# gMLP z2 in nine groups of eight column units, with batch-norm statistics for its mean and variance

## The chip, the cores and the metric

One core of one Trainium2 chip runs the whole program. The metric is the device time of one execution in microseconds (us), start to end, lower is better. The core has five engines that run their own instruction streams and wait for each other by semaphores: TensorE (PE in the profile, with its weight loads as PEld), VectorE (DVE), ScalarE (ACT), GpSimd (POOL) and SyncE (SP, which here only starts transfers). Matrix products land in PSUM, which has eight banks of 512 float32 columns; everything else lives in SBUF, 128 partitions wide.

## The reference

Four layers, A B A B, on x of 2048 rows and 576 columns. A is a dilated local attention; B is a gated MLP (gMLP). The change is inside B only:

```python
def _layernorm(x, axis=-1, eps=1e-05):
    m = jnp.mean(x, axis=axis, keepdims=True)
    v = jnp.var(x, axis=axis, keepdims=True)
    return (x - m) / jnp.sqrt(v + eps)

def _B_ref(x, w_in, w_sp, b_sp, w_out):
    B, S, D = x.shape                      # 1, 2048, 576
    F = w_in.shape[-1]                     # 4608
    Fh = F // 2                            # 2304
    z = _gelu(jnp.einsum('bsd,df->bsf', x, w_in))
    z1 = z[..., :Fh].copy()
    z2 = _layernorm(z[..., Fh:], axis=-1)
    g = jnp.einsum('ts,bsf->btf', w_sp, z2) + b_sp[None, :, None]
    return jnp.einsum('bsf,fd->bsd', z1 * g, w_out)

x = x + _B_ref(_layernorm(x, axis=-1), B_w_in, B_w_sp, B_b_sp, B_w_out)
```

So z2 is, for every one of the 2048 rows, 2304 columns of Gelu of a product with 576 terms, then normalized over those 2304 columns.

## The kernel before

`layer_B` runs three phases. The first makes z2 and stores its normalized form in `Z`; the second walks over nine pairs of feature blocks, and for each makes z1 (`z1`) and multiplies `Z` by w_sp (`gate`); the third multiplies by w_out. Only the first phase is changed, lines 778 to 876.

**Tiles.** Rows go in 16 row tiles of 128 (`NS`). The 576 terms go as chunks c = 0 to 3 of 128, full height on the array, and c = 4, the last 64. In `xnT` and `win2` the last chunk stands twice, in partitions 0 to 63 and 64 to 127, so that two half-height matmuls can use the two halves of the array; `z_mm` (L814) gives each of them its half by `tile_position`. The 2304 columns of a row tile are four units of 512 and one of 256, in three PSUM allocations: two `H_tile`s of two banks (`pz`) and one `PT_tile` of one bank (`pzs`). There are two H buffers and four PT buffers, together the eight banks.

**Order on TensorE for a row tile** (L822 to L829): the full-height chunks of units 0 and 1, then chunk 4 of all five units (a lone one stays over), then the full-height chunks of units 2 to 4.

**Behind it.** ACT empties the banks by Gelu into `zp` (L831; 1024, 1024 and 256 columns), with running sums in `z_sums`. For the mean square, DVE squares the first 1536 columns (L833) and ACT the other 768 (L835, Square); both write the squares into `spare`, the tenth block of `Z`, and keep only the sums. Five one-column operations on DVE (L838 to L846) make mean and variance, POOL takes the power -1/2 (L848) and makes -mean x rstd (L850). `p1_norm` writes the normalized row: DVE 2048 columns (L858), POOL the last 256 (L860). It is called for row i-1 after row i's main part.

**Buffers.** `zp` has three buffers, so row i's first Gelu waits for both norms of row i-3. `Z` takes over memory in which the attention layer keeps `stg`, from which the last transposes into `xnT` (L252, helper `ln_T`) still read when phase one begins. The space of `zp` is used again by the second phase (w1, `z1T`, `g_tmp`).

**Order.** The attention layer's instructions are issued in a hand-set order (`manual_schedule`); layer B's are put in order by the framework's scheduler. SP's queue holds, in order: the last transposes into `xnT`, the first w1 load, the four transposing loads of w_sp (L777, `Wq`), then more w1. POOL's queue holds the last LayerNorm rows of the attention (L245), the load of the gate's bias (`bsp`, L80, which reuses the buffers `ln_xn` that the last transposes read), then row 0's rstd and so on. `run_deferred` issues the last row's transpose.

In the second phase, one z1 block (L907) is eight units of 512 columns with the same chunks: four units' full-height chunks, chunk 4 of all eight, the other four units' full-height chunks. A gate (L931) reads all 16 row tiles of `Z`, row 15 in its sixteenth matmul.

Of the kernel before, what the change touches and what calls it, by code (L numbers as in the profile page):

```python
# [9 lines left out]
ACT = mybir.ActivationFunctionType  # L10
ALU = mybir.AluOpType
AX = mybir.AxisListType
f32 = mybir.dt.float32
bf16 = mybir.dt.bfloat16
# [4 lines left out]
P = 128  # L19
# [7 lines left out]
PADL = 16  # L27
KO = PADL - HALO
EPS = 1e-5
# [36 lines left out]
class K:  # L66
# [682 lines left out]
    def layer_B(self, li):  # L749
        nc, tc, cfg = self.nc, self.tc, self.cfg  # L750
        S, NS, Fh, NJ, NB, NQ = cfg.S, cfg.NS, cfg.Fh, cfg.NJ, cfg.NB, cfg.NQ
# [7 lines left out]
        Z = zu_cm.__enter__().tile([P, NB + 1, NS, 256], bf16, name="Z")  # L759
        spare = Z[:, NB].rearrange("p a b -> p (a b)")  # L760
# [8 lines left out]
        p1 = p1_cm.__enter__()  # L769
# [3 lines left out]
        def win2(c):  # L773
            return win2a[:, c, :] if c < NPF else win2b[:, c - NPF, :]

        def load_W(q):
            nc.sync.dma_start_transpose(out=Wq[q][:], in_=self.B_w_sp[q * 512:(q + 1) * 512, :])  # L777
        cchunks = []
        c0 = 0
        while c0 < Fh:  # L780
            cn = min(1024, Fh - c0)
            cchunks.append((c0, cn))
            c0 += cn
        ncch = len(cchunks)
        SQ_D = (Fh * 2 // 3) // 256 * 256
        units = []
        for ci, (c0, cn) in enumerate(cchunks):
            for sub in range((cn + 511) // 512):
                units.append((ci, c0, sub, min(512, cn - sub * 512)))
        bsp = self.bsp  # L790
        w1_0 = spare[:, Fh:Fh + 1280].rearrange("p (c n) -> p c n", n=256)
        p2s = []
# [2 lines left out]
        def load_w1(jj):  # L795
            w1 = w1_0 if jj == 0 else p2s[0].tile([P, 5, 256], bf16, name="w1")
            w1s[jj] = w1
            cs = slice(jj * 256, (jj + 1) * 256)
            self.dma(w1[:, 0:4, :], self.B_w_in[0:512, cs].rearrange("(c p) n -> p c n", p=P), eng=nc.sync)
            for r in (0, 64):  # L800
                self.dma(w1[r:r + 64, 4, :], self.B_w_in[512:576, cs], eng=nc.sync)
        zst = {}

        def p1_main(i):
            zp = p1.tile([P, Fh], bf16, name="zp", bufs=3)
            sums = p1.tile([P, ncch + 2], f32, name="z_sums", bufs=3)
            pzvs = []
            for ci, (c0, cn) in enumerate(cchunks):
                if cn > 512:
                    pzvs.append(self.H_tile("pz")[:].rearrange("p a b -> p (a b)"))  # L810
                else:
                    pzvs.append(self.PT_tile([P, 512], f32, "pzs")[:, :])

            def z_mm(u, c, start, stop):  # L814
                ci, c0, sub, w = units[u]
                r0, r1 = (0, P) if c < 4 else (64 * (u % 2), 64 * (u % 2) + 64)
                nc.tensor.matmul(pzvs[ci][:, sub * 512:sub * 512 + w],  # L817
                                 lhsT=self.xnT[r0:r1, c, PADL + i * P:PADL + (i + 1) * P],
                                 rhs=win2(c)[r0:r1, c0 + sub * 512:c0 + sub * 512 + w],
                                 start=start, stop=stop, tile_position=(r0, 0))  # L820
            nu = len(units)
            for u in range(2):  # L822
                for c in range(4):
                    z_mm(u, c, c == 0, False)
            for u in range(nu):
                z_mm(u, 4, u >= 2, u < 2)
            for u in range(2, nu):
                for c in range(4):
                    z_mm(u, c, False, c == 3)  # L829
            for ci, (c0, cn) in enumerate(cchunks):  # L830
                nc.scalar.activation(out=zp[:, c0:c0 + cn], in_=pzvs[ci][:, 0:cn],  # L831
                                     func=ACT.Gelu_apprx_tanh, accum_out=sums[:, ci:ci + 1])
            nc.vector.tensor_tensor_reduce(out=spare[:, 0:SQ_D], in0=zp[:, 0:SQ_D], in1=zp[:, 0:SQ_D], scale=1.0,  # L833
                                           scalar=0.0, op0=ALU.mult, op1=ALU.add, accum_out=sums[:, ncch:ncch + 1])
            nc.scalar.activation(out=spare[:, SQ_D:Fh], in_=zp[:, SQ_D:Fh], func=ACT.Square,  # L835
                                 accum_out=sums[:, ncch + 1:ncch + 2])
            mean = p1.tile([P, 1], f32, name="z_mean", bufs=3)
            nc.vector.tensor_reduce(out=mean[:], in_=sums[:, 0:ncch], axis=AX.X, op=ALU.add)  # L838
            nc.vector.tensor_scalar_mul(out=mean[:], in0=mean[:], scalar1=1.0 / Fh)
            msq = p1.tile([P, 1], f32, name="z_msq", bufs=3)  # L840
            nc.vector.scalar_tensor_tensor(out=msq[:], in0=mean[:], scalar=mean[:, 0:1], in1=self.eps_t[:],
                                           op0=ALU.mult, op1=ALU.subtract)
            sq = p1.tile([P, 1], f32, name="z_sq", bufs=3)
            nc.vector.tensor_tensor(out=sq[:], in0=sums[:, ncch:ncch + 1], in1=sums[:, ncch + 1:ncch + 2], op=ALU.add)
            rstd = p1.tile([P, 1], f32, name="z_rstd", bufs=3)
            nc.vector.scalar_tensor_tensor(out=rstd[:], in0=sq[:], scalar=1.0 / Fh, in1=msq[:],  # L846
                                           op0=ALU.mult, op1=ALU.subtract)
            nc.gpsimd.tensor_tensor(out=rstd[:], in0=rstd[:], in1=self.neg_half[:], op=ALU.pow)  # L848
            nmr = p1.tile([P, 1], f32, name="z_nmr", bufs=3)
            nc.gpsimd.tensor_scalar(out=nmr[:], in0=mean[:], scalar1=rstd[:, 0:1], scalar2=-1.0,  # L850
                                    op0=ALU.mult, op1=ALU.mult)
            zst[i] = (zp, mean, rstd, nmr)

        def p1_norm(i):
            zp, mean, rstd, nmr = zst.pop(i)
            nb = NB - 1
            zv = zp[:].rearrange("p (b c) -> p b c", c=256)
            nc.vector.tensor_scalar(out=Z[:, 0:nb, i, :], in0=zv[:, 0:nb, :], scalar1=mean[:, 0:1],  # L858
                                    scalar2=rstd[:, 0:1], op0=ALU.subtract, op1=ALU.mult)
            nc.gpsimd.tensor_scalar(out=Z[:, nb, i, :], in0=zv[:, nb, :], scalar1=rstd[:, 0:1],  # L860
                                    scalar2=nmr[:, 0:1], op0=ALU.mult, op1=ALU.add)

        for i in range(NS):
            self.run_deferred(upto_row=(i + 1) * P)
            p1_main(i)
            if i == 0:
                self.run_deferred()
            if i == min(2, NS - 1):
                for q in range(NQ):
                    load_W(q)  # L870
                load_w1(0)
            if i == min(6, NS - 1):
                self.dma(bsp, self.B_b_sp.partition_broadcast(P), eng=nc.gpsimd)
            if i >= 1:
                p1_norm(i - 1)
        p1_norm(NS - 1)
        p1_cm.__exit__(None, None, None)
        self.right["pf_cm"].__exit__(None, None, None)
        self.right = None
# [114 lines left out]
        if NS >= 2 and JL > 0:  # L994
            accs = []
            for i in range(2):
                ht = self.H_tile("po2")
# [87 lines left out]
```

## Time and profile before

| What | us |
|---|---|
| median of three runs | 1185.04 |
| the three runs | 1183.01, 1185.39, 1185.04 |
| the profiled execution | 1182.29 |
| its span on the core | 1180.5 |
| first gMLP layer: first pz matmul, first z1 matmul | 127.93, 204.56 |
| second gMLP layer: the same | 709.94, 786.12 |
| one z1 block (40 matmuls) | 7.99 |

The profile is of one execution. A row of the table of groups reads: source line, engine, operation, what it writes and reads with shapes, count; then the total busy time and the mean of one in ns; then the idle time of the engine just before these instructions and what ended it. A timeline row begins with start and length in us; idle time before it and its releaser stand in brackets. "PEq" and the like are the engines' sequencers. The order of instructions on each engine, which the prediction also uses, is that of the built programs.

### The profile page before, as it was taken

Reading aid. Unit: us, or ns where it says so; the run is one execution under the profiler, and the core shown is the slowest. Engines: PE = TensorE matmul, PEld = TensorE weight load, DVE = VectorE, ACT = ScalarE, POOL = GpSimd, SP = SyncE. Lnnn points to the kernel's source line nnn. Section 1 sums busy time; section 2 is a strip of 40 time slices with the busy share of each in tenths; the row PEclk is TensorE's granted clock in tenths of the full one; section 3 lists DMA queues with packets and bytes.
Section 4 is the critical chain, followed back from the end, with each engine's and each line's share of the span. In section 5 each row is a group of like instructions: output and inputs, shape, how many; then the busy total and the mean of one; then the engine's idle time right before and its main releaser. Section 6 shows DMA issues by size and latency. Waiting matters only on the chain.

```text
span 1180.5 us, 20534 instructions
## 1 busy us (share of the span) xinstructions
PE 1169.8 (99%) x8406; PEld 622.2 (53%) x8406; DVE 553.0 (47%) x1232; ACT 377.3 (32%) x621; POOL 285.8 (24%) x383
## 2 busy tenths in 40 slices
PE   9999999999999999999999999999999999999998
PEld 5567544444444444457755774444444444444677
DVE  9778677323333322335556896753322333332321
ACT  5588677111110111102257786770111110111000
POOL 4768784000000000001153787830000000000000
PEclk9999999999999999999999999999999999999999
DMA  8999993000000000049645899900000000001332
GB/s 200 199 136 235 197 206 70 23 12 12 12 1 12 12 12 1 18 145 282 170 99 116 201 245 175 223 23 1 12 12 12 12 3 10 12 1 39 114 106 74
DMA packets 179479, 101.57 MB, mean 86 GB/s; under 512 B 135711, under 2 KB 160735, under 8 KB 179384
## 3 DMA queue, kind: packets, MB, share of 16 engines
q1 hardware_dynamic: 166520, 78.50, 31.2%
q0 software_dynamic: 6512, 16.00, 5.2%
q10 hardware_dynamic: 6352, 5.75, 1.6%
q8 instruction: 66, 1.08, 0.4%
q14 instruction: 29, 0.24, 0.1%
HBM read 42.39 MB, written 16.53 MB: 50 GB/s over the span
## 4 chain that ended last, share of the span: by engine, by line
PE 89%; POOL 4%; DMA 2%; DVE 2%; issue 1%; ACT 1%; SPq 0%; POOLq 0%; ACTq 0%; DVEq 0%
PE pg L931 42%; PE po L973 12%; PE pz L817 9%; PE pz L907 6%; PE pz1s L907 6%; PE pp L409 4%; PE pv L386 2%; PE O_ps L464 2%; PE L_ps L444 2%; POOL ln_xn L245 2%; PE pw L509 2%; PE pzs L817 1%; DMA o_slot<-o_t 1%; DMA QK<-win2a 1%; POOL QK L80 1%
## 5 line engine op out<-in xcount | busy, mean ns | idle before, releaser
L931 PE MATMUL pg<-Wq,Z 128*128 128x512 bf16 x2304 | 500.2, 379 | 0.0
L931 PEld LDWEIGHTS <-Z 128*128 128x128 bf16 x2304 | 225.4, 98 | 271.9
L935 DVE TENSOR_TENSOR g_tmp<-pg,ln_xn 128x512 f32<-128x512 f32 x144 | 99.6, 692 | 422.2 <-PE pg L931 422.2
L926 ACT ACTIVATE z1T<-pz 128x1024 bf16<-128x1024 f32 x36 | 34.9, 1020 | 497.4 <-PE pz L907 493.8
L80 POOL DMA_DIRECT2D wout<-in_B_w_out_dram x4 | 4.2, 1062 | 600.8 <-PE pg L931 600.8
L973 PE MATMUL po<-wout,Z 128*128 128x288 bf16 x1152 | 141.4, 286 | 0.0
L453 ACT ACTIVATE P_sb<-L_ps 128x912 bf16<-128x912 f32 (+1 forms) x144 | 125.7, 929 | 36.2 <-PE L_ps L444 35.3
L973 PEld LDWEIGHTS <-Z 128*128 128x128 bf16 x1152 | 112.7, 98 | 28.8
L817 PEld LDWEIGHTS <-xnT 128*128 128x128 bf16 (+1 forms) x800 | 66.5, 97 | 83.3 <-issue 25.6
L936 DVE TENSOR_TENSOR Z<-g_tmp,z1T 128x512 bf16<-128x512 f32 x144 | 99.7, 692 | 13.0 <-DVE g_tmp L935 0.9
L817 PE MATMUL pz<-win2a,xnT 128*128 128x512 bf16 x384 | 104.1, 380 | 1.5 <-ACT zp L831 1.5
L907 PEld LDWEIGHTS <-w 128*128 128x128 bf16 (+1 forms) x640 | 53.8, 97 | 74.0 <-issue 13.6
L409 PE MATMUL pp<-xnT,wqk_sb 128*128 128x512 bf16 x360 | 82.5, 379 | 0.0
L831 ACT ACTIVATE zp<-pz 128x1024 bf16<-128x1024 f32 x64 | 65.5, 1023 | 36.8 <-PE pz L817 31.1
L983 DVE TENSOR_TENSOR x_new<-po,xo 128x288 f32<-128x288 f32 (+1 forms) x64 | 28.8, 456 | 87.7 <-PE po L973 84.0
L907 PE MATMUL pz<-xnT,w 128*128 128x512 bf16 (+1 forms) x320 | 66.5, 380 | 0.0
L907 PE MATMUL pz1s<-xnT,w 128*128 128x512 bf16 (+1 forms) x320 | 66.5, 379 | 0.0
L817 PE MATMUL pz<-win2b,xnT 128*128 128x512 bf16 (+1 forms) x256 | 65.7, 380 | 0.0
L80 POOL DMA_DIRECT2D QK<-stg x81 | 50.9, 633 | 50.9 <-DVE oT L483 17.9
L833 DVE CUSTOM_DVE_ANT_0 Z<-zp 128x1536 bf16<-128x1536 bf16 x32 | 56.9, 1778 | 11.5 <-ACT zp L831 7.1
L386 PE MATMUL pv<-wv_sb,xnT 128*128 128x288 bf16 (+1 forms) x360 | 52.8, 286 | 1.1 <-DVE o_t L471 1.0
L245 POOL TENSOR_SCALAR ln_xn<-x_new,ln_mv,ln_rstd 128x576 bf16<-128x576 f32 x23 | 53.0, 2303 | 2.0
(118 smaller groups left out, 1002.2 us busy)
## 6 DMA issues: line engine op xcount, KB each, us to landing
xres<-x_new SPq DMA_DIRECT2D x48, 288.0 KB
xo<-xres SPq DMA_DIRECT2D x32, 288.0 KB
wout<-in_B_w_out_dram POOLq DMA_DIRECT2D x4, 1296.0 KB, 8.6
xo<-xres SPq DMA_DIRECT2D x8, 576.0 KB
w<-in_B_w_in_dram SPq DMA_DIRECT2D x16, 256.0 KB
QK<-stg POOLq DMA_DIRECT2D x53, 72.0 KB, 4.3
QK<-stg SPq DMA_DIRECT2D x41, 72.0 KB
xo<-in_A_x_dram SPq DMA_DIRECT2D x8, 288.0 KB
```

What stands on the lines that cost most here:

```text
L80: return eng.dma_start(out=out, in_=in_)
L245: e.tensor_scalar(out=xn[:nrows, 0:D], in0=x_t[:nrows, :], scalar1=mv[:nrows, 0:1], scalar2=rstd[:nrows, 0:1], op0=ALU.subtract, op1=ALU.mult)
L386: nc.tensor.matmul(pv[:nk, 0:288], lhsT=self.xnT[:, c, KO + q0_(t):KO + q0_(t) + nk], rhs=wv_sb[:, c, hh * 288:(hh + 1) * 288], start=(c = ...
L409: nc.tensor.matmul(pp[:, :], lhsT=w, rhs=self.xnT[:, c, PADL + cc * 512:PADL + (cc + 1) * 512], start=(c == 0), stop=(c == 4))
L453: nc.scalar.activation(out=P_bufs[(2 * s + jp) % 4][:nk, :, :, 0:nq], in_=Lv[:nk, :, :, 0:nq], func=ACT.Exp, scale=scale)
L817: nc.tensor.matmul(pzvs[ci][:, sub * 512:sub * 512 + w], lhsT=self.xnT[r0:r1, c, PADL + i * P:PADL + (i + 1) * P], rhs=win2(c)[r0:r1, c0 + ...
L831: nc.scalar.activation(out=zp[:, c0:c0 + cn], in_=pzvs[ci][:, 0:cn], func=ACT.Gelu_apprx_tanh, accum_out=sums[:, ci:ci + 1])
L907: nc.tensor.matmul(outs[a_], lhsT=w1[r0:r1, c, sub * P:(sub + 1) * P], rhs=self.xnT[r0:r1, c, PADL + q * 512:PADL + (q + 1) * 512], start= ...
L931: nc.tensor.matmul(pg[:, :], lhsT=Z[:, jj, i, sub * P:(sub + 1) * P], rhs=Wq[q][:, i, :], start=(i == 0), stop=(i == NS - 1))
L935: nc.vector.tensor_tensor(out=tmp[:], in0=pg[:, :], in1=bsp[:, qs], op=ALU.add)
L936: nc.vector.tensor_tensor(out=uT(jj)[:, sub, qs], in0=tmp[:], in1=z1Ts[jj, sub][:, qs], op=ALU.mult)
L973: nc.tensor.matmul(acc[hh], lhsT=uT(j // 2)[:, j % 2, i * P:(i + 1) * P], rhs=wouts[j // NJH][:, j % NJH, hh * 288:(hh + 1) * 288], start= ...
```

## The change

The 16 row tiles are taken in pairs. A pair's columns form a stream of nine units of 512: four of the first row, one mixed unit that holds the last 256 columns of both rows side by side in one bank, and four of the second row. The stream of 72 units is cut into nine groups of eight, one unit for each PSUM bank, wherever the row borders lie. In a group, the first four units lie in the two H tiles and the others in the four PT tiles. TensorE does the full-height chunks of the first four units (and of the mixed unit's first part, if it lies later), then chunk 4 of all eight, then the rest. The mixed unit's two parts both use the upper half of the array for chunk 4.

Gelu takes 512 columns at a time, 1024 where units 0 and 1 or 2 and 3 of a group belong together in one row, 256 for the mixed unit's parts; it keeps no running sums. After each, DVE takes batch-norm statistics of the 512 (or 256) columns just written. After a row's five sets DVE aggregates them into mean and variance, and POOL adds EPS and takes the power. Squares, sums and the small DVE operations are gone. A row's norm is issued on DVE after two further statistics (`owed`); both DVE's and POOL's parts subtract the mean and multiply by rstd. DVE and ACT run this phase in the order in which the code issues it (`manual_schedule`). The w_sp loads are issued after the second group, the bias load after the fourth; in the built programs the SP queue and the rest of POOL's queue have the same order as before, and outside this phase so have all engines.

```diff
-        cchunks = []
...
-        units = []
-        for ci, (c0, cn) in enumerate(cchunks):
-            for sub in range((cn + 511) // 512):
-                units.append((ci, c0, sub, min(512, cn - sub * 512)))
...
-        def p1_main(i):
...
-            for u in range(2):
-                for c in range(4):
-                    z_mm(u, c, c == 0, False)
-            for u in range(nu):
-                z_mm(u, 4, u >= 2, u < 2)
-            for u in range(2, nu):
-                for c in range(4):
-                    z_mm(u, c, False, c == 3)
-            for ci, (c0, cn) in enumerate(cchunks):
-                nc.scalar.activation(out=zp[:, c0:c0 + cn], in_=pzvs[ci][:, 0:cn],
-                                     func=ACT.Gelu_apprx_tanh, accum_out=sums[:, ci:ci + 1])
-            nc.vector.tensor_tensor_reduce(out=spare[:, 0:SQ_D], in0=zp[:, 0:SQ_D], in1=zp[:, 0:SQ_D], scale=1.0,
-                                           scalar=0.0, op0=ALU.mult, op1=ALU.add, accum_out=sums[:, ncch:ncch + 1])
-            nc.scalar.activation(out=spare[:, SQ_D:Fh], in_=zp[:, SQ_D:Fh], func=ACT.Square,
-                                 accum_out=sums[:, ncch + 1:ncch + 2])
...
+        NW, MW = Fh // 512, Fh % 512
+        stream = []
+        for r in range(0, NS, 2):
+            stream += [(r, w_) for w_ in range(NW)] + [("m", r)] + [(r + 1, w_) for w_ in range(NW)]
+        groups = [stream[k_:k_ + 8] for k_ in range(0, len(stream), 8)]
+        zrow, zst = {}, {}
+        left = {r: NW + 1 for r in range(NS)}
+
+        def unit_parts(u):
+            if u[0] == "m":
+                return [(u[1], NW * 512, 0, MW), (u[1] + 1, NW * 512, MW, MW)]
+            return [(u[0], u[1] * 512, 0, 512)]
...
+        def p1_group(units):
...
+            mk = [k_ for k_, u in enumerate(units) if u[0] == "m"]
+            for k_ in list(range(4)) + [k_ for k_ in mk if k_ >= 4]:
                 for c in range(4):
-                    z_mm(u, c, c == 0, False)
...
+                    z_mm(units[k_], bank(k_), c, 0, c == 0, False)
+            half = 0
+            for k_, u in enumerate(units):
+                if u[0] != "m":
+                    z_mm(u, bank(k_), 4, half % 2, k_ >= 4, k_ < 4)
+                    half += 1
+            for k_ in mk:
+                for part in range(2):
+                    z_mm(units[k_], bank(k_), 4, 1, part == 1, part == 0, part)
+            for k_ in [k_ for k_ in mk if k_ < 4] + list(range(4, len(units))):
                 for c in range(4):
...
+                    z_mm(units[k_], bank(k_), c, 0, False, c == 3, 1 if units[k_][0] == "m" else 0)
+            for r, w0, (k_, o0), n in evictions(units):
+                if r not in zrow:
+                    zrow[r] = (p1.tile([P, Fh], bf16, name="zp", bufs=3),
+                               p1.tile([P, NW + 1, nc.vector.BN_STATS_DIM], f32, name="z_st", bufs=3))
+                zp, st = zrow[r]
+                t_, o_ = outs[k_]
+                nc.scalar.activation(out=zp[:, w0:w0 + n], in_=t_[:, o_ + o0:o_ + o0 + n], func=ACT.Gelu_apprx_tanh)
+                for x in range(w0, w0 + n, 512):
+                    nc.vector.bn_stats(out=st[:, x // 512, :], in_=zp[:, x:x + min(512, w0 + n - x)])
+                    left[r] -= 1
+                    for o in owed:
+                        o[1] -= 1
+                    while owed and owed[0][1] <= 0:
+                        p1_norm(owed.pop(0)[0])
+                if left[r] == 0:
+                    p1_stats(r)
+                    owed.append([r, 2])
+
+        def p1_stats(i):
+            zp, st = zrow.pop(i)
+            mv = p1.tile([P, 2], f32, name="z_mv", bufs=3)
+            nc.vector.bn_aggr(out=mv[:], in_=st[:])
             rstd = p1.tile([P, 1], f32, name="z_rstd", bufs=3)
...
+            nc.gpsimd.tensor_scalar(out=rstd[:], in0=mv[:, 1:2], scalar1=EPS, scalar2=None, op0=ALU.add)
             nc.gpsimd.tensor_tensor(out=rstd[:], in0=rstd[:], in1=self.neg_half[:], op=ALU.pow)
...
         def p1_norm(i):
-            zp, mean, rstd, nmr = zst.pop(i)
+            zp, mv, rstd = zst.pop(i)
...
+            for eng, b0, b1 in ((nc.vector, 0, nb), (nc.gpsimd, nb, NB)):
+                eng.tensor_scalar(out=Z[:, b0:b1, i, :], in0=zv[:, b0:b1, :], scalar1=mv[:, 0:1],
+                                  scalar2=rstd[:, 0:1], op0=ALU.subtract, op1=ALU.mult)
...
+        p1_man = tc.manual_schedule(engines={ET.DVE, ET.Activation})
+        p1_man.__enter__()
+        for k_, units in enumerate(groups):
+            self.run_deferred(upto_row=(max(r for u in units for r, _, _, _ in unit_parts(u)) + 1) * P)
+            p1_group(units)
...
+        while owed:
+            p1_norm(owed.pop(0)[0])
+        p1_man.__exit__(None, None, None)
```

## Prediction

> **What bounds the kernel now.** I read the page's first part, then the chain of waits, then the two stretches of the z2 phase in the table of windows.
>
> ```profile
> PE 1169.8 (99%) x8406; PEld 622.2 (53%) x8406; DVE 553.0 (47%) x1232; ACT 377.3 (32%) x621; POOL 285.8 (24%) x383
> PE 89%; POOL 4%; DMA 2%; DVE 2%; issue 1%; ACT 1%; SPq 0%; POOLq 0%; ACTq 0%; DVEq 0%
> ```
>
> TensorE is busy or waited for everywhere; only what shortens its queue, or makes it wait, shows in the end. The table of windows (columns: span, then busy time of each engine) has, in order: z2 phase of the first gMLP layer from its first pz matmul to the first z1 matmul; the same in the second; its undisturbed last 14 rows; the first z1 block of each layer; a later z1 block.
>
> ```profile
> 127.93:204.56 76.63, 75.65 (x415) 34.19 (x411) 54.19 (x137) 55.97 (x125) 51.99 (x56) 1.00 0.85 156
> 709.94:786.12 76.18, 75.65 (x414) 34.23 (x411) 54.55 (x137) 56.13 (x125) 53.49 (x56) 1.00 0.74 150
> 139.60:204.56 64.96, 64.96 (x351) 29.12 (x350) 47.39 (x117) 49.48 (x113) 40.91 (x45) 1.00 0.82 146
> 204.56:212.54 7.98, 7.98 (x42) 3.36 (x40) 3.54 (x9) 5.80 (x11) 2.81 (x5) 1.00 0.12 33
> 240.18:248.17 7.99, 7.99 (x42) 3.37 (x41) 1.39 (x2) 3.62 (x5) 0.00 (x0) 1.00 0.00 0
> ```
>
> A row tile costs 64.96/14 = 4.64 us, and the granted clock is 1.00. A z1 block is what a new z2 group is: eight 512-column units, each of four full-height matmuls and a half-height one, the eight half-height ones together: 7.99 us. Inside one row (timeline of TensorE; start, length):
>
> ```profile
> 735.95 0.81 PE L817 MATMUL pz<-win2a,xnT 128*128 128x512 bf16 x3
> 736.59 0.92 PE L817 MATMUL pz<-win2b,xnT 128*128 128x512 bf16 x5
> 737.35 0.27 PE L817 MATMUL pzs<-win2b,xnT 64*128 64x256 bf16 x1
> 737.55 0.39 PE L817 MATMUL pz<-win2a,xnT 128*128 128x512 bf16 x1
> ```
>
> Three 512-column matmuls start 0.64 us apart, so 0.215 each. From 736.59 to 737.55 lie one of these, two pairs of half-height ones (a pair takes one slot) and a lone 256-column one (0.11): 0.75 us of streaming in 0.96. So going to half height and back costs 0.2 us.
>
> **TensorE's part of the change.** Before, 16 rows x 4.64 = 74.24 us a layer. After, 9 groups x 7.99 = 71.91. In the eight groups with a mixed unit, eight 256-column matmuls (0.11 each) replace four 512s (0.865): +0.015 each, 0.12 in all. Sum 72.03; gain 2.21 a layer, from 9 height changes for 16 and no lone 256s. The ten pw matmuls of the attention tail stay after the first four pz in both orders (130.05-127.93-0.86 = 1.26 us).
>
> What is left of the two stretches is waiting: 76.63-74.24-1.26 = 1.13 and 76.18-74.24-1.25 = 0.69 us. The first one's cause:
>
> ```profile
> 137.61 0.84 ACT L835 ACTIVATE Z<-zp 128x768 bf16<-128x768 bf16 x1 [2.55 <-DMA xnT<-stg]
> ```
>
> Square writes into Z, whose memory the last transposes out of stg still read; ACT's later Gelus queue behind it, and 0.98 us of TensorE idleness follows. Without squares, only DVE's first norm waits for that memory. In the second layer (0.53 us of it in one wait) ACT was late because DVE stood behind row 0's rstd, which stays: see below. I take both waits as gone: 1.13 + 0.69 = 1.82; with 2 x 2.21 that is 6.24 us. For one late bank per layer I keep 0.1 back each: 6.0.
>
> **What must keep up, ACT.** A row had two 1024-wide Gelus, a 256, Square and four accumulator reads: 49.48/14 = 3.53 us busy. Now no Square and no reads, but more pieces: by the z1T rows a 512 costs 0.60, a 1024 1.02, a 256 0.38. The costliest group (seven 512s and a mixed unit, none merged) is 7 x 0.60 + 2 x 0.38 = 4.96 us of 7.99. Cover: 3 us a group.
>
> **DVE** takes 4.5 statistics a row instead of a squaring pass and five one-column operations. Groups (count | busy, mean ns | idle before):
>
> ```profile
> L833 DVE CUSTOM_DVE_ANT_0 Z<-zp 128x1536 bf16<-128x1536 bf16 x32 | 56.9, 1778 | 11.5 <-ACT zp L831 7.1 <-DMA xnT<-stg 4.4
> L220 DVE BATCH_NORM_STATS2 ln_st<-x_new 128x6 f32<-128x288 f32 x96 | 40.4, 450 | 0.9
> L569 DVE BATCH_NORM_STATS2 ln_st<-x_in 128x6 f32<-128x288 bf16 x24 | 9.6, 442 | 0.0
> L858 DVE TENSOR_SCALAR Z<-zp,z_mean,z_rstd 128x2048 bf16<-128x2048 bf16 x32 | 26.0, 813 | 31.0 <-POOL z_rstd L848 31.0
> L222 DVE BATCH_NORM_AGGREGATE ln_mv<-ln_st 128x2 f32<-128x12 f32 x48 | 10.0, 209 | 4.3
> L936 DVE TENSOR_TENSOR Z<-g_tmp,z1T 128x512 bf16<-128x512 f32 x144 | 99.7, 692 | 13.0 <-DVE g_tmp L935 0.9
> ```
>
> No row shows statistics of 512 columns. From below: as long as 288, 0.44 us. From above: in proportion, 0.45 x 512/288 = 0.80. Between: 512 against 288 columns of tensor_tensor cost 692 against 458 ns (L471), 1.04 ns a column, so 442 + 224 x 1.04 = 0.68; 256 columns 0.41. I take this, the nearest slope. bf16 and f32 cost the same at 288, so no faster mode for 16 bits shows. Aggregation 0.21 (two sets; I take 0.25 for five). Two rows: 8 x 0.68 + 2 x 0.41 + 2 x 0.25 + 2 x 0.81 = 8.4 us, against TensorE's 9/8 x 7.99 = 8.99. It fits, with 0.6 to spare, at the cheap end with 2.5, and at 0.80 it doesn't by 0.5 (9.48, with 0.47 for the 256s).
>
> [...]
>
> DVE runs in a hand-set order: a norm stands after two further statistics, and behind it wait all later statistics, then ACT by the three zp buffers, then TensorE by a PSUM bank. Between aggregation and norm POOL adds EPS (0.27, as L229) and takes the power (0.55, L848), about 1.0 us with hand-overs; two statistics cover 1.09 to 1.36. Without that cover each row would add up to 1.0 us to DVE.
>
> **Opening.** POOL's order is unchanged: the bias broadcast sits ahead of row 0's rstd.
>
> ```profile
> 142.76 0.64 POOL L80 DMA_DIRECT2D ln_xn<-in_B_b_sp_dram  x1 [3.18 <-DMA xnT<-ln_xn]
> 143.43 0.59 POOL L848 TENSOR_TENSOR z_rstd<-z_rstd,neg_half 128x1 f32<-128x1 f32 x1
> L850 POOL TENSOR_SCALAR z_nmr<-z_mean,z_rstd 128x1 f32<-128x1 f32 x32 | 25.4, 794 | 3.3
> L229 POOL TENSOR_SCALAR ln_nmr<-ln_mv,ln_rstd 128x1 f32<-128x1 f32 x16 | 4.3, 266 | 1.6
> ```
>
> The same POOL operation takes 794 ns beside DVE's norm and 266 elsewhere: POOL is held while the norm runs. Counted from the first pz: POOL free at 15.5 (second layer 15.8), add and power to 16.4, DVE's norm to 17.2, POOL's 256 columns (0.56 to 1.95 in L860's rows) to 17.8 or 19.2. Row 3's first Gelu waits for that buffer and ends 0.6 later, 18.4 to 19.8. Its bank is wanted by the mixed unit of the third group, at 1.26 + 2 x 8.0 + 3.46 = 20.7. Margin 0.9 to 2.3 us, so no stall or a tenth.
>
> **Close.** With T the last group's end, the last Gelu ends at T+0.8, statistics 0.7, aggregation 0.25, POOL 0.8, norm 0.8: T+3.7 with hand-overs, T+6 if DVE is three statistics behind. The gate starts at T+7.99 and wants row 15 in its 16th matmul, T+11.2. SP keeps its order; the w_sp transposes are issued by 183.9 and 762 in the profile, over 20 us before gates read them, and the next w1 load has a whole 35 us block.
>
> **Sum.** The profiled execution took 1182.29 us (span 1180.5); 1182.29 - 6.0 = 1176.3. The three runs' median, 1185.04, lies 2.75 higher; against it 1179.0.
>
> **Rivals.** (1) Only the streaming gain comes, and less: the mixed unit's two 256s use the same half of the array and may not both run beside their 512 partner (for: the lone 256 cost 0.11 before; against: pairs share a slot), 8 x 0.11 a layer; and the opening waits stay, as row 0's rstd is as late as before. 6.24 - 1.76 - 1.82 = 2.7: 1182.4. (2) DVE becomes the bound. For: its spare is 0.6 us in 9, and proportional statistics don't fit. Against: 288 columns show a large fixed part. Place: statistics behind each other, felt at the zp buffers and the first gate. From the opening's 17.2 about 14.5 rows remain; TensorE wants the last norm at 73.3 + 11.2 = 84.5. Break-even is a stall of 3.1 a layer, (87.6-17.2)/14.5 = 4.86 a row, two rows 9.7, statistics at 0.82 us. At 0.87 with 0.51 for the 256s, two rows take 10.1, the end is 90.4, stall 5.9, net +2.8 a layer: 1190.6. (3) That the order on TensorE isn't as grouped is excluded: the built order shows groups of eight.
>
> **Chances.** Forecast 0.70 (own range 1176.5 to 1181.5), rival 1 0.18, rival 2 0.12. A measurement can tell about 0.2%, 2.4 us. Rival 1 gives a third of its chance to faster: 0.76; same 0.12; slower 0.12. The range goes down to 1175.5, as the runs lie 2.4 us apart, and up to 1186.5, which takes in rival 1 and DVE costs up to break-even.
>
> **What would show it.** The z2 stretches at 73.3 us each; a group every 8.0; no TensorE idleness put down to ACT in them; statistics of 512 columns near 0.68; norms waiting under 0.3 us for rstd after row 2. It is wrong if zp's Gelus wait for norms through the whole phase, or a group takes over 8.2.

## The result, and the profile after

The changed kernel takes 1177.79 us (median of six runs, 1175.84 to 1178.95) against 1184.17 for the kernel before beside it (1181.56 to 1185.39): a ratio of 0.9946, 95% interval 0.9931 to 0.9962. A second series, later, gave 1177.90 against 1185.30, ratio 0.9945 (0.9929 to 0.9961). The profiled execution of after took 1178.62 us, its span 1176.3.

First the page's first part and its chain of waits, of the changed kernel:

```profile
PE 1160.3 (99%) x8309; PEld 623.0 (53%) x8406; DVE 569.3 (48%) x1200; ACT 340.3 (29%) x501; POOL 278.2 (24%) x383
PE 92%; DMA 2%; DVE 2%; issue 1%; POOL 1%; ACT 1%; DVEq 0%; SPq 0%; POOLq 0%
```

TensorE is the bound as before, and its share of the chain grew. (x8309 instead of x8406 matmuls are records missing from the trace, not work: the weight loads are all 8406.) Now the table of windows, columns as in the prediction: the two z2 stretches and the z1 block behind the first.

```profile
128.20:201.40 73.20, 72.72 (x405) 35.04 (x412) 60.46 (x122) 39.14 (x69) 47.25 (x55) 1.00 0.90 162
708.72:781.92 73.20, 72.72 (x406) 35.01 (x411) 60.46 (x122) 39.14 (x69) 47.28 (x55) 1.00 0.74 153
201.40:209.38 7.98, 7.98 (x40) 3.35 (x40) 4.45 (x8) 4.22 (x6) 5.07 (x6) 1.00 0.02 4
```

The stretches were 76.63 and 76.18. They are now 73.20 and 73.20, a gain of 3.43 + 2.98 = 6.41 us; the medians differ by 6.38 (by 7.40 in the second series). Two further traces of the changed kernel, below, show 73.20 four more times: TensorE waits for nothing in this phase any more, and its time doesn't vary. (In the first trace the record of the very first pz matmul is missing in both layers; its start is one slot of 0.22 us before the second's, and the traces with that record give the same 73.20. The same record is missing in the traces of the experiments, all but the one with extra POOL operations; the stretches given there include the 0.22.)

The timeline of TensorE in the first group shows the middle of a group, with its mixed unit:

```profile
132.91 0.49 PE L807 MATMUL pzs<-win2a,xnT 128*128 128x256 bf16 x3
133.24 0.27 PE L807 MATMUL pzs<-win2b,xnT 128*128 128x256 bf16 x1
133.44 0.60 PE L807 MATMUL pz<-win2b,xnT 64*128 64x512 bf16 x4
133.88 0.60 PE L807 MATMUL pzs<-win2b,xnT 64*128 64x512 bf16 x5
134.41 0.50 PE L807 MATMUL pzs<-win2a,xnT 128*128 128x256 bf16 x3
```

From 133.44 to 134.41 lie seven half-height 512s and two half-height 256s (the record shows them in one run of five): 0.97 us, of which four slots of streaming are 0.86. Ahead of them, 0.20 us pass from the last full-height matmul of 256 columns, which needs 0.11, to the first half-height one: 0.11 us on the way back and 0.09 on the way in, the 0.2 us of a height change. One such stay at half height per group, where the kernel before had one per row.

The other engines, from the table of groups with shapes kept apart:

```profile
L856 DVE BATCH_NORM_STATS2 z_st<-zp 128x6 f32<-128x512 bf16 x128 | 81.1, 674 | 8.5 <-ACT zp L854 8.3
L856 DVE BATCH_NORM_STATS2 z_st<-zp 128x6 f32<-128x256 bf16 x32 | 12.5, 391 | 2.1 <-ACT zp L854 2.1
L869 DVE BATCH_NORM_AGGREGATE z_mv<-z_st 128x2 f32<-128x30 f32 x32 | 9.3, 291 | 1.1
L880 DVE TENSOR_SCALAR Z<-zp,z_mv,z_rstd 128x2048 bf16<-128x2048 bf16 x32 | 25.8, 806 | 15.3 <-POOL z_rstd L872 13.5
L880 POOL TENSOR_SCALAR Z<-zp,z_mv,z_rstd 128x256 bf16<-128x256 bf16 x32 | 55.8, 1742 | 3.4
```

A statistics instruction of 512 columns takes 674 ns, and the norms of 32 rows waited 13.5 us in all for rstd. The timeline of DVE shows where:

```profile
144.65 0.81 DVE L880 TENSOR_SCALAR Z<-zp,z_mv,z_rstd 128x2048 bf16<-128x2048 bf16 x1 [5.70 <-POOL z_rstd L872]
145.38 1.87 DVE L856 BATCH_NORM_STATS2 z_st<-zp 128x6 f32<-128x512 bf16 x3
147.28 0.29 DVE L869 BATCH_NORM_AGGREGATE z_mv<-z_st 128x2 f32<-128x30 f32 x1
147.49 1.22 DVE L856 BATCH_NORM_STATS2 z_st<-zp 128x6 f32<-128x512 bf16 x2
148.63 0.80 DVE L880 TENSOR_SCALAR Z<-zp,z_mv,z_rstd 128x2048 bf16<-128x2048 bf16 x1
...
152.28 0.81 DVE L880 TENSOR_SCALAR Z<-zp,z_mv,z_rstd 128x2048 bf16<-128x2048 bf16 x1
```

The one long wait (5.70 us, and the like in the second layer) is the opening: row 0's rstd stands on POOL behind the bias load. After that DVE is behind and works almost without a pause (every other norm waits 0.13 us); its norms start at 144.65, 148.63, 152.28, 156.26, 159.91, so two rows cost 7.63 us, against TensorE's 8.99. Three statistics take 1.87 us, since each starts 0.60 us after the one before although it is 0.67 long.

**What lies outside the phase.** In the first pair of profiles the spans differ by 4.2 us only, less than the 6.41 gained. From the first z1 matmul of the first gMLP layer to the first pz matmul of the second, code that the change doesn't touch, before took 505.4 us and after 507.3. Other traces with the same code there: 506.3 (before, second trace), 507.5 and 506.0 (after, second and third trace). So this part scatters by about 2 us between executions, whatever the kernel.

### The profile page after: what moved, and what is told of

It reads as the page before. It is cut to its first block, busy times and chain, and to the rows that moved or that the text cites. A ratio compares the mean times of both kernels' runs of the same rounds, so it can differ in the third digit from the quotient of the medians.

```text
span 1176.3 us, 20282 instructions
## 1 busy us (share of the span) xinstructions
PE 1160.3 (99%) x8309; PEld 623.0 (53%) x8406; DVE 569.3 (48%) x1200; ACT 340.3 (29%) x501; POOL 278.2 (24%) x383
## 4 chain that ended last, share of the span: by engine, by line
PE 92%; DMA 2%; DVE 2%; issue 1%; POOL 1%; ACT 1%; DVEq 0%; SPq 0%; POOLq 0%
PE pg L955 42%; PE po L997 12%; PE pz L807 6%; PE pz L931 6%; PE pz1s L931 6%; PE pzs L807 6%; PE pp L409 5%; PE pv L386 3%; PE pw L509 2%; PE O_ps L464 2%; PE L_ps L444 2%; DMA o_slot<-o_t 2%; DMA QK<-win2a 1%; POOL QK L80 1%; ACT P_sb L453 1%
## 5 line engine op out<-in xcount | busy, mean ns | idle before, releaser
L856 DVE BATCH_NORM_STATS2 z_st<-zp 128x6 f32<-128x512 bf16 (+1 forms) x160 | 91.1, 618 | 10.6 <-ACT zp L854 10.4
L807 PE MATMUL pzs<-win2a,xnT 128*128 128x512 bf16 (+1 forms) x234 | 58.5, 358 | 0.3
L807 PE MATMUL pz<-win2a,xnT 128*128 128x512 bf16 (+1 forms) x234 | 58.5, 357 | 0.3
L880 POOL TENSOR_SCALAR Z<-zp,z_mv,z_rstd 128x256 bf16<-128x256 bf16 x32 | 55.8, 1742 | 3.4
```

Source lines behind the costliest of these rows:

```text
L807: nc.tensor.matmul(out[:, o0:o0 + n], lhsT=self.xnT[r0:r1, c, PADL + r * P:PADL + (r + 1) * P], rhs=win2(c)[r0:r1, w0:w0 + n], start=start ...
L856: nc.vector.bn_stats(out=st[:, x // 512, :], in_=zp[:, x:x + min(512, w0 + n - x)])
L880: eng.tensor_scalar(out=Z[:, b0:b1, i, :], in0=zv[:, b0:b1, :], scalar1=mv[:, 0:1], scalar2=rstd[:, 0:1], op0=ALU.subtract, op1=ALU.mult)
```

## The experiments

**Halves of the change.** Statistics alone: the kernel before, its rows in its order on TensorE, with the new Gelu, statistics and norm.

```diff
-                nc.scalar.activation(out=zp[:, c0:c0 + cn], in_=pzvs[ci][:, 0:cn],
-                                     func=ACT.Gelu_apprx_tanh, accum_out=sums[:, ci:ci + 1])
-            nc.vector.tensor_tensor_reduce(out=spare[:, 0:SQ_D], in0=zp[:, 0:SQ_D], in1=zp[:, 0:SQ_D], scale=1.0,
...
+                nc.scalar.activation(out=zp[:, c0:c0 + cn], in_=pzvs[ci][:, 0:cn], func=ACT.Gelu_apprx_tanh)
+                for x in range(c0, c0 + cn, 512):
+                    nc.vector.bn_stats(out=st[:, x // 512, :], in_=zp[:, x:x + min(512, c0 + cn - x)])
...
+            p1_stats(i)
+            owed.append([i, 2])
```

> The row-by-row order on TensorE of before with the statistics, norms and hand-set DVE and ACT order of after. Theory (the gain is TensorE's own: 2.2 us a layer from fewer height changes and no lone 256-column halves, and 1.8 us in all from waits that the squares caused): the row pace stays 4.64 us, the two z2 stretches become 16 x 4.64 + 1.26 = 75.5 us each instead of 76.6 and 76.2, the time falls by about 1.8 us to 1182.4 (before: 1184.2). Rival (the gain comes from the lighter DVE and ACT work, the grouping adds little): most of the 6.4 us comes here, 1178 to 1179.

Measured: 1182.69 us, ratio to before 0.9982 (0.9966 to 0.9997); both stretches 75.5 us, no wait of TensorE in them. The ends of the first one, from the timeline of TensorE (75.27 us and the missing 0.22):

```profile
127.63 0.59 PE L818 MATMUL pz<-win2a,xnT 128*128 128x512 bf16 x2
...
202.90 4.16 PE L907 MATMUL pz<-xnT,Z 128*128 128x512 bf16 x20
```

That is 74.24 + 1.26: the waits of 1.13 and 0.69 us are gone without the groups, and streaming is as before. The edit also brings the hand-set order of DVE and ACT, which was not tried by itself.

Groups alone: the changed kernel's order on TensorE, with the squares, sums and old norm.

```diff
+                nc.scalar.activation(out=zp[:, w0:w0 + n], in_=t_[:, o_ + o0:o_ + o0 + n], func=ACT.Gelu_apprx_tanh,
+                                     accum_out=sums[:, j:j + 1])
...
+            nc.vector.tensor_tensor_reduce(out=spare[:, 0:SQ_D], in0=zp[:, 0:SQ_D], in1=zp[:, 0:SQ_D], scale=1.0,
...
+            nc.scalar.activation(out=spare[:, SQ_D:Fh], in_=zp[:, SQ_D:Fh], func=ACT.Square,
```

> The nine groups of after with the running sums, squares, small operations and scheduler's order of before. Theory: TensorE could run 73.2 us a stretch, but ACT needs about 4.2 us of Gelu, 1.5 of accumulator reads and 1.8 of squares in each group of 8.0, 7.5 in all, so it falls behind and TensorE waits for banks; stretches between 74 and 77 us, time 1179 to 1185, with TensorE idleness put down to ACT. Rival (the statistics are the gain): no better than before, 1184, whatever TensorE's order.

Measured: 1180.64 us, 0.997 (0.9955 to 0.9986); stretches 74.45 and 74.2, that is 1.25 and 1.0 above 73.20, with TensorE waiting for Gelus. All of it arises at one place in each layer, at the half-height matmuls of the third group (150.96 and 732.59), where the Gelus stand behind row 0's late norm; ACT doesn't fall behind in every group, as the expectation had it. So the two halves gain 1.13 and 0.68 (statistics) and 2.2 and 2.0 (groups), 6.0 of 6.41 us; each is worth having by itself, and the last 0.4 us come only with both.

**The price of a height change.** The changed kernel with two stays at half height in each group.

```diff
-            for k_ in list(range(4)) + [k_ for k_ in mk if k_ >= 4]:
...
+            for ks in (range(0, 4), range(4, len(units))):
+                for k_ in ks:
+                    for c in range(4):
+                        z_mm(units[k_], bank(k_), c, 0, c == 0, False)
...
+                        z_mm(u, bank(k_), 4, half % 2, False, True)
```

> After, but chunk 4 of units 0 to 3 and of units 4 to 7 in two separate places of each group: as many matmuls of each form, one more change to half height and back per group. Theory: 0.2 us a change, 9 a layer, stretches 73.2 + 1.8 = 75.0 us each, time +3.6: 1181.4. Rival (the height change is free, the old row lost its time to the lone 256s alone): no change, 1177.8.

Measured: 1181.64 us, 0.9983 (0.9974 to 0.9992), both stretches 75.1 (74.87 and the missing 0.22):

```profile
129.07 0.59 PE L807 MATMUL pz<-win2a,xnT 128*128 128x512 bf16 x2
...
203.94 4.16 PE L931 MATMUL pz<-xnT,Z 128*128 128x512 bf16 x19
```

That is 1.9 us for nine more changes, 0.21 us each, with no wait of TensorE. The 0.2 us read from one timeline in the prediction is the price.

**No cover.** A row's norm directly behind its aggregation on DVE.

```diff
-                    owed.append([r, 2])
+                    p1_norm(r)
```

> After, but each norm directly behind its aggregation on DVE, without the two statistics between. Theory: DVE waits about 1.0 us for POOL's add and power in every row, its row grows from 3.8 to 4.8 us against TensorE's 4.49; it ends some 4 to 5 us later, T+10 instead of T+5.6, still ahead of the gate's sixteenth matmul at T+11.2, so the time stays within 1 us of after's. Rival (the cover lies on the path): 16 us a layer, over 1190.

Measured: 1200.38 us, in one execution. This expectation was far off, and the run was the most useful of all. DVE now waits 1.0 us for rstd in each row, and its norms start 4.855 us apart (151.38, 156.23, 161.09): just over TensorE's 4.49. From the timelines of TensorE and ACT in this kernel:

```profile
202.43 0.37 PE L807 MATMUL pzs<-win2b,xnT 64*128 64x512 bf16 x1 [1.04 <-ACT zp L854]
218.82 4.00 PE L955 MATMUL pg<-Wq,Z 128*128 128x512 bf16 x9 [4.01 <-ACT z1T L950]
216.34 1.94 ACT L950 ACTIVATE z1T<-pz 128x1024 bf16<-128x1024 f32 x2 [7.36 <-POOL Z L880]
```

and from its table of windows, behind the first gate matmul:

```profile
218.82:223.04 4.22, 4.00 (x10) 1.43 (x11) 0.81 (x1) 1.42 (x3) 2.23 (x2) 0.50 0.11 31
```

Three losses in each layer. First the stretch is 76.62 us, 3.4 longer (rows fall behind until the zp buffers run out). Then the first gate waits 4.0 us, not for row 15's norm: z1T lies in the space of zp, its first Gelu waited for POOL's norm of row 14 (which ended at 216.30), and the gate needs a PSUM bank that this Gelu and the next ones empty. Then the gate matmuls run at about half speed, the granted clock in that window being 0.50, and not only there: the 21st recorded one starts 7.26 us behind the first (7.12 in the second layer), against 4.53 in the changed kernel, so 2.7 and 2.6 us are lost. The gate comes 4.2 us late in all. Sum 3.4 + 4.2 + 2.7 = 10.3 and 3.4 + 4.2 + 2.6 = 10.2, together 20.5 of the 22.3 us by which the span is longer than that of the changed kernel (1198.6 against 1176.3); the other 1.8 lie outside the change, as this execution reached its first pz matmul 1.8 us later.

**The margin.** With that, two theories of the close stood against each other: the prediction's (row 15's norm is wanted by the gate's sixteenth matmul, T+11.2) and the new one (row 14's norm on POOL is wanted by z1T). The first pair of runs adds statistics whose results nobody reads, one and two of 512 columns a row.

```diff
                     nc.vector.bn_stats(out=st[:, x // 512, :], in_=zp[:, x:x + min(512, w0 + n - x)])
+                    if x < 512:
+                        nc.vector.bn_stats(out=z_dm[:, x // 512, :], in_=zp[:, x:x + 512])
```

> The changed kernel with one extra 512-column statistics instruction in each row tile, whose result nobody reads. By start-to-start times of the changed kernel's trace VectorE's row goes from 3.82 to 3.82 + 0.62 = 4.44 us, just under TensorE's 4.49. Theory A (the deadline at the close is the z1T buffers, which take the memory of zp: row 14's norm on GpSimd must end by about T+5.0, T being the first z1 matmul, as two z1T Gelus of 1.94 us and one of 0.6 stand between it and the first gate): the lag of the opening no longer shrinks, row 14's norm ends near T+7.2, so the first gate matmul comes about 2 us late in each layer: 1178 + 4 to 1178 + 8 (with a slow clock behind the wait), 1182 to 1187; the z2 stretches stay under 73.8 us. Theory B (the prediction's accounting: two rows of 8.9 us fit in 8.99, and the close wants only row 15 at T+11.2): no change, 1177 to 1180, and no wait ahead of the first gate.

Measured: 1178.24 us, 0.9933 (0.9908 to 0.9959), both stretches 73.20, no gate late: no change. Theory A's number was wrong because an extra statistic costs less than 0.62 us: norms start at 147.79, 156.37, 164.95, two rows in 8.58 us, so 0.48 for each extra. The trace accounts for it: an extra one starts the next instruction 0.59 us later, and 0.21 us in two rows come back in front of every other norm, which had started 0.80 us behind the statistics ahead of it (152.28, behind statistics that ended at 152.15 in the changed kernel) and now starts 0.59 behind: 2 x 0.59 - 0.21 = 0.97. With the true row, row 14's POOL norm ends at T+4.4, and theory A too asks for no wait.

With two (`x < 1024`):

> The changed kernel with two extra 512-column statistics in each row tile. VectorE's row is 3.82 + 2 x 0.62 = 5.06 us against TensorE's 4.49: VectorE is the bound. Theory B (the prediction's rival 2: last norm at 17.2 + 14.5 x 5.06 = 90.6 after the first pz, wanted at 84.4): 6.2 us lost in each layer, 1190 to 1192. Theory A (z2 stretch longer by 15 x 0.57 less about 2.1 us that three zp buffers take up, 6.5 us; then a wait of 4 us at the first gate for the z1T buffers, and about 2 us of matmuls at half clock behind it, as in the run without cover): 12 to 13 us lost in each layer, 1202 to 1206.

Measured: 1198.45 us, in one execution. Rows take 4.89 us; stretches 76.84 and 76.89; the first gate waits 3.42 us and the next 14 recorded gate matmuls take 4.97 us instead of 3.40, at a granted clock of 0.61 in the 4.16 us from 219.34. Theory B's 1190 to 1192 is out. Theory A's 1202 to 1206 is high, by its 5.06 us a row for 4.89; its three losses are all there.

Next, the norm after one further statistic instead of two.

```diff
-                    owed.append([r, 2])
+                    owed.append([r, 1])
```

> The changed kernel with a row's norm placed after one further statistics instruction instead of two. GpSimd's add and power take 0.80 us, 1.0 with hand-overs; one statistics covers 0.62, so VectorE should wait about 0.4 us in front of each norm, a row of 3.82 + 0.4 = 4.2 us, still under TensorE's 4.49: theory (cover is needed only as far as VectorE's row stays under TensorE's): no change, 1177 to 1180, z2 stretches 73.2. Rival (GpSimd's own row, which is held during VectorE's norm and slow beside its statistics, is what counts, and any missing cover shows): stretches over 74 and the first gate waiting, 1182 or more.

Measured: 1180.56 us, 0.9951 (0.9934 to 0.9968), whose interval covers the changed kernel's ratio. Stretches 73.20; DVE waits 0.45 and 0.72 us in turn, two rows take 8.78 us, still under 8.99. But the first gate waits 0.90 and 0.95 us, which the expectation had given to the rival, and the median lies just above its 1177 to 1180: row 14's POOL norm ends at T+6.5. Of the rival's two reasons one fails: POOL's part of a norm takes 1.76 us with statistics of DVE beside it (from 206.64) and without (from 211.16). The other fits: it takes 1.23 in the changed kernel where no norm of DVE runs beside it (from 196.96).

```profile
210.91 13.33 PE L955 MATMUL pg<-Wq,Z 128*128 128x512 bf16 x59 [0.90 <-ACT z1T L950]
```

Last, no cover for rows 0 to 11 and the changed kernel's for rows 12 to 15.

```diff
-                    owed.append([r, 2])
+                    if r < NS - 4:
+                        p1_norm(r)
+                    else:
+                        owed.append([r, 2])
```

> The changed kernel with the norm directly behind its aggregation (no cover) for rows 0 to 11, and after two further statistics, as in the changed kernel, for rows 12 to 15. Twelve rows of 4.855 us fall behind TensorE's 4.49 by 4.4 us, 2.1 of which the zp buffers take up; the last four rows, at 3.82, win back 2.7. Theory A (deadline at the z1T buffers): stretches near 75.5 us, row 14's norm 2 to 3 us nearer to T than in the run without any cover (T+9.7), so a first gate that waits 1 to 2 us instead of 4.0; 1184 to 1188 if the clock stays at 1.00 behind so short a wait, about 4 more if it drops as there. Theory B (the loss of the run without cover comes from the stretch and the clock, not from a deadline at z1T): first gate still 4 us late or not late at all, with the stretch unchanged at 76.6.

Measured: 1188.23 us, 1.0023 (1.0011 to 1.0036). The gates wait 1.95 and 1.94 us, as theory A said, and the clock stays at 1.00. The stretches are 76.5, as without any cover, and not 75.5: the last bank that TensorE waits for in the phase holds row 14's first columns, and their Gelu waits for row 11's norm, the last one without cover; the four fast rows help only what follows.

The six kernels settle the close. T is the first z1 matmul of the first gMLP layer:

| kernel | T | row 14's POOL norm ends | first gate matmul | gate behind norm | gate behind T |
|---|---|---|---|---|---|
| changed | 201.40 | 204.11 (T+2.7) | 209.38 | 5.27 | 7.98 |
| one extra statistic | 199.94 | 204.35 (T+4.4) | 207.93 | 3.58 | 7.99 |
| norm after one | 201.86 | 208.40 (T+6.5) | 210.91 | 2.51 | 9.05 |
| cover for the last four | 204.81 | 212.40 (T+7.6) | 214.91 | 2.51 | 10.10 |
| two extra statistics | 207.78 | 216.83 (T+9.1) | 219.34 | 2.51 | 11.56 |
| no cover | 206.66 | 216.30 (T+9.6) | 218.82 | 2.52 | 12.16 |

In all four that are late, the first gate comes 2.51 us behind that norm: two z1T Gelus of 1024 columns in 1.94, and the first 512 of the next z1T, which empties a bank. So the deadline is T + 7.98 - 2.51 = T+5.5, and the changed kernel keeps it by 2.8 us.

**The opening.** Six extra operations on POOL that read zp of row 0, meant to stand ahead of row 0's rstd.

```diff
+            if i == 0:
+                for _ in range(6):
+                    nc.gpsimd.tensor_scalar(out=z_dm[:], in0=zp[:, 0:256], scalar1=mv[:, 0:1], scalar2=None, op0=ALU.subtract)
```

> The changed kernel with six extra 256-column operations on GpSimd ahead of row 0's rstd, so that row 0's norm comes about 3.3 us later (six of 0.56 us, the duration of such an operation alone). In the changed kernel's trace row 3's first Gelu ends at 146.9 and its bank is wanted again at 148.9, a margin of 2.0 us. Theory (the opening has that one deadline and VectorE wins the lag back afterwards, 0.67 us a row): TensorE waits 1.2 to 1.5 us once, at the third group's mixed unit, in each layer; stretches 74.4 to 74.7, the first gate not late; 1180 to 1181.5. Rival (the lag is passed on to the close, or the margin is larger than the trace shows): either a first gate that waits as well, 1183 or more, or stretches of 73.2 and 1178.

Measured: 1185.64 us, 1.0021 against before (1.0000 to 1.0042); stretches 77.98 and 77.82; gates in time. From the timelines of ACT and TensorE, and then the windows behind the wait:

```profile
150.48 1.36 ACT L855 ACTIVATE zp<-pzs 128x256 bf16<-128x256 f32 x3 [7.13 <-POOL z_dm L874]
150.91 1.37 PE L808 MATMUL pzs<-win2b,xnT 64*128 64x512 bf16 x5 [2.16 <-ACT zp L855]
152.22 1.46 PE L808 MATMUL pzs<-win2a,xnT 128*128 128x512 bf16 x3
```

```profile
150.91:154.00 3.09, 2.86 (x10) 0.98 (x10) 2.64 (x6) 2.65 (x4) 2.14 (x2) 0.72 1.29 108
154.00:158.00 4.00, 4.00 (x18) 1.81 (x17) 3.83 (x8) 2.48 (x6) 2.55 (x3) 0.79 1.19 187
```

The edit did not do quite what it was to do: the scheduler put two of the six before row 0's power and the other four behind it, three of these behind row 0's norm, and each took 0.93 to 1.26 us, not 0.56. So row 3's buffer came free by the last extra operation at 150.45, 23.5 us after the first pz matmul, instead of 18.3: 5.25 late, not 3.3. TensorE waited 2.16 us, which puts the margin at 5.25 - 2.16 = 3.1 us. In the changed kernel itself row 3's first Gelu ends at 146.9 and the half-height matmuls into the PT banks start at 149.87: 3.0. The wait is in front of those, and the mixed unit's full-height matmuls before them (147.61 here) ran on time. Theory holds in that the wait comes once and the gate is not late; its size is over twice the wait, as the clock fell behind it (0.72 and 0.79 in the two windows): from 150.91 to the next group's start at 156.94 is 6.03 us, where the changed kernel takes 3.57. In the second layer the wait is 2.31 us.

**Second traces.** The unchanged kernels again.

> The kernel before once more, for a second trace. The profiled executions of before and after differ by 3.67 us, while the two z2 stretches got 6.41 us shorter. If the rest is scatter of the second attention layer between executions, the time from the first layer's first z1 matmul to the second layer's first pz matmul, 505.4 us in the first trace of before and 506.4 to 507.9 in the traces of the others, is here within 506 to 508; if the change made that part longer, it is again at 505.4.

> The changed kernel once more, for a second trace. Stretches 73.2 and 73.2 again, the first gate not late; the time between the stretches 506 to 508 us, whatever its cause.

> The changed kernel timed again beside the kernel before, in more executions. The single look at it gave 1182.42 us with both z2 stretches at 73.2, the excess lying in the first attention layer (first pz matmul at 132.4 instead of 128.2). If that was scatter of one execution, the median is again 1176 to 1180 and the ratio inside 0.993 to 0.996; if the first timing was lucky, the median is 1180 or more and the ratio above 0.997.

Before: 1184.69 us, stretches 77.18 and 76.19, 506.3 us between them, so 505.4 in the first trace is no property of that kernel. After: one execution of 1182.42 us with stretches of 73.20 and 73.20; its first pz matmul came at 132.4 instead of 128.2, behind more waits in the first attention layer. The series of six runs that followed (1175.63 to 1180.03, median 1177.90) and its profile, 1175.63 us with stretches of 73.20 and 73.20, show that as one execution's scatter.

## Why the prediction was right, and where it was not

- **TensorE's row and group.** Right. 16 x 4.64 = 74.24 is what the statistics alone leave. The changed stretch less the pw matmuls is 73.20 - 1.26 = 71.94 for a forecast of 72.03; nine groups of 7.99 are 71.91. In the third trace of the changed kernel a group with a mixed unit takes 7.995 us and the fifth group, which has none, 7.984: 0.011 us for a mixed unit, 0.09 in all, where the prediction had 0.015 and 0.12.
- **The opening waits, 1.82 us.** Right: gone in the kernel with the statistics alone (76.63 to 75.5, 76.18 to 75.5). The 0.1 us held back in each layer wasn't needed: 6.24 computed, 6.41 found. Whether writing the squares elsewhere would by itself have ended the first layer's wait was not tried, and neither was the hand-set order by itself.
- **Rival 1** fell with both of its parts: the mixed unit's 256s cost 0.01 us a group and not 0.11, and the waits went. **DVE's statistics** at 0.68 us: 0.674 measured, the nearest slope was the right choice between 0.44 and 0.80. With 391 ns for 256 columns and 674 for 512, a column costs 1.11 ns and about 0.11 us are fixed, an estimate from these two lengths. Aggregation 0.29 for 0.25.
- **DVE's two rows, 8.4 us**: mis-sized, 7.63. An instruction here starts before the one ahead has ended (statistics 0.60 us apart for a length of 0.674), and the sum took full lengths. This was to the safe side; the spare is 1.36 us in two rows, not 0.6.
- **ACT**, with cover of 3 us a group: right, 39.14 us in nine groups, 4.35 each.
- **Cover of 1.0 us a row** on POOL's hand-over: right as a cost on DVE (4.855 - 3.815 = 1.04), and norms indeed waited under 0.3 us with it (0.13), all but the last row's, behind which no statistics stand (1.0).
- **Opening margin, 0.9 to 2.3 us**: mis-sized, 3.0. It was put at the mixed unit's full-height matmuls, and the first matmuls to wait are the half-height ones 0.97 us later.
- **POOL's 256 columns, 0.56 to 1.95 us**: 1.74 as a mean, near the upper bound.
- **Close**: the step that failed. It looked at the gate's operand, row 15 at T+11.2, and not at the memory: "The space of zp is used again" stood in the description of the kernel, and the deadline from it is T+5.5. That this did no harm is luck, as nothing in the sum asked for it. It would have done none at the forecast pace either: with one extra statistic two rows take 8.58 us, more than the 8.4 forecast, and row 14's norm still ends at T+4.4.
- **Rival 2's price** therefore was wrong. Its break-even of 4.86 us a row is the row of the run without cover, and that took 1200 us, 16 over before. The limit is near TensorE's own 4.49: at 4.39 (norm after one statistic) nothing is lost in the stretch and about 1 us at the gate, at 4.89 it is 9 us a layer (3.65 + 3.58 + 1.7 for the slow clock).

**The sum.** 1176.3 was forecast for the profiled execution, which took 1178.62: of the 2.3 us, 1.9 are the untouched middle part (507.3 against 505.4), 0.3 lie ahead of the first pz matmul and 0.5 outside the span, less the 0.4 by which the gain exceeded the forecast. Against the medians the change is worth 6.4 us in the first series and 7.4 in the second, the forecast 6.0.

## What to carry to other kernels

Where one engine is the bound at a full clock, price its stream from a timeline (here 0.2 us for each change of height, 0.11 for a lone piece) and count how often each occurs; such a sum holds to 0.1 us in 73. For what must keep up, compare cost per period with the bound's period first, and only then look for deadlines; a deadline can lie in reused memory well before the reader of the result. The waits of 2.16 to 4.02 us on TensorE cost their length here and 1.6 to 2.7 us more, most or all of it for the clock behind them (0.72 to 0.50 in the first layer); those of 0.90 to 1.95 us at the gate left it at 1.00.

## What the runs showed of the hardware

**The clock behind a wait.** TensorE waits of 0.90 and 0.95 us (norm after one statistic) and of 1.95 and 1.94 (cover for the last four rows) left the granted clock at 1.00. Behind waits of 2.16 (extra POOL operations), 3.42 (two extra statistics) and 4.01 (no cover) it was 0.72, 0.61 and 0.50 as a mean of the 3 to 4 us behind them. The rows of two of these, windows that begin with the first matmul after the wait:

```profile
214.91:219.00 4.09, 4.04 (x18) 1.85 (x19) 0.78 (x2) 1.42 (x3) 1.42 (x1) 1.00 0.26 75
```

```profile
219.34:223.50 4.16, 4.10 (x11) 1.56 (x12) 0.81 (x1) 1.42 (x3) 2.56 (x3) 0.61 0.02 5
```

In 4 us, 18 matmuls run behind a wait of 1.95 (first fence, cover for the last four rows) and 11 behind 3.42 (second fence, two extra statistics).

The lowest granted clock of these windows is the 0.50 without cover (218.82 to 223.04, and 809.61 to 813.90 in the second layer). Behind the extra POOL operations full-height matmuls of 512 columns start 0.42 us apart from 152.22 to 155.60, eight of them in 3.38 us, and 0.22 apart again from 156.07 on.

What the windows fall short of 1.00 gives an estimate of how long the clock was at 0.50. With the extra POOL operations it is 0.28 x 3.09 + 0.21 x 4.00 = 1.71 us in the first layer and 0.43 x 3.56 + 0.05 x 3.50 = 1.71 in the second (735.44 to 739.00 at 0.57, then to 742.50 at 0.95); with two extra statistics 0.01 x 8.33 + 0.39 x 4.16 = 1.71 (the first term from 211.00 to 219.33, ahead of the gate) and 0.30 x 2.90 + 0.18 x 4.60 = 1.70 (808.50 to 811.40 at 0.70, then to 816.00 at 0.82). That is 3.4 us at 0.50 each time. Without cover it is about twice as much: 0.95 in the 12.16 us up to the first gate matmul and 0.90 in the 27.18 us from it, 0.61 + 2.72 = 3.33 us, so 6.7 us at 0.50, the first of it during the wait.

The length of the longest wait doesn't decide it everywhere. In the first 60 us the granted clock was 0.97 in the second trace of the kernel before and 1.00 in the first trace of the changed kernel, and 1.00 in both from there to 128 us. TensorE's longest waits in the first 133 us were 1.5 us (ahead of the program's first matmul) and 0.8 in the former, 1.5 and 1.1 in the latter. What does decide it was not shown.

**Statistics overlap.** Batch-norm statistics of 512 bf16 columns are 0.674 us long in the trace of the changed kernel, and start 0.60 us apart when they stand in a row.
